# Batches 0 and 1 of an attention and channel-mixing kernel: q by runs of tokens, tokens rotated by one, v cast by its load, mixed weights in one step

## The chip, the cores and the metric

The kernel runs on one core of one Trainium2 chip. The metric is the device time of one execution in microseconds (us); where several runs are compared, the median counts.

## The reference

Linear attention, and then a channel-mixing layer that blends each token with the one before it. There are 8 batches of 576 tokens, 8 heads of 64 features, so 512 features a token, and 1024 hidden features.

```python
q_s = softmax(q, over the 64 features of a head)      # each token by itself
k_s = softmax(k, over the 576 tokens)                 # each feature by itself
kv  = einsum('bhsd,bhse->bhde', k_s, v)                # 64x64 a head
x   = q_s @ kv, heads side by side                    # (8, 576, 512)

x_prev = x moved by one token, zero first
xk = mu_k * x + (1 - mu_k) * x_prev
xr = mu_r * x + (1 - mu_r) * x_prev
k  = relu(xk @ w_k)
v  = (k * k) @ w_v
out = sigmoid(xr @ w_r) * v
```

Inputs and output are float32; the kernel multiplies in bfloat16 and adds up in float32.

## The kernel before

**Tiling.** A batch is worked on in two groups g (0 and 1). A group holds the heads 2g, 2g+1, 2g+4 and 2g+5: one pair of heads lies on the two halves of the 128 partitions (the code's r), the other pair is the second half of the free dimension (u). Each partition holds nine tokens in a row (j = 0 to 8), so token t is at partition t // 9, run j = t % 9, and after the transposes column 64 j + t // 9. A neighbour in time is thus 64 columns away, except for j = 0, whose predecessor is run 8, one partition up: a small copy, the edge, puts those 63 columns in front.

**Attention of batches 0 and 1 ("fused").** For batch b and group g the operations are, by the names that stand in the order list: `load` q, k and v (two halves n by u); `expq`, `rsum`, `rrec`, `scale` make softmaxed q (`qs`); `T` transposes it on PE into PSUM, and `qt` copies it to SBUF, one half by ACT and one by DVE; `edge` copies the last 63 columns to the front; `expk` makes exp of k; `KV` multiplies it with v on PE, and `Z` (a column of ones) gives the sums for k's softmax in batch 0, while in batch 1 a 65th column of v does that; `rz` is the reciprocal; `kvn` divides; `wp` multiplies kv by mu and by 1-mu, so that `X` on PE gives the mixed xk (m = 0) and xr (m = 1) straight away, in two parts t of 288 tokens; `x` copies them out to `xk` or `xr`. Batch 0's v is loaded with a cast to bfloat16 into a tile `vbs`, batch 1's v is loaded as float32 and cast on GpSimd (`cast`).

**Attention of batches 2 to 7** makes x plain and mixes it on DVE (`TKV`, `B`, `X` on PE, `diff`, `sc`, `mix` on DVE). It isn't touched but for its places in the order.

**Channel mixing.** Columns are taken in units (`UNITS`, two rings of 2304 tokens). For unit i and hidden tile fc, `k{i}_{fc}` multiplies xk with w_k, `relu` on ACT and `sq` on DVE square it. A unit of 256 columns takes two hidden tiles in one PSUM bank. In the early units each k is split in two: the first half needs group 0's xk and w_k tile `wk{h}0`, the second (".2") group 1's and `wk{h}1`. For each tile m of 128 tokens, `r{m}` multiplies xr with w_r, `th` is the tanh that gives the sigmoid, `v{m}_{part}` multiplies with w_v, `o` gates, `st` stores. PSUM has four banks `mm` for these and two pairs `att` for attention; a slot `any` is an `att` pair or two `mm` banks.

**The order.** Every engine works its instructions strictly in the order of one list written out by hand, `ORDER`. A token `name:2` puts the result in buffer 2, `name^other` makes it wait for another operation, `ACT!name` puts it on that engine. A buffer is given again only when its last user is done. `fill` is a matmul of zeros that nobody reads. Each engine's queue blocks at its first waiting instruction. Loads of batch 0 are on the DMA queues of SP and ACT, the weights and later batches on GpSimd's (POOL); stores are on SP.

Of the kernel before, what the change touches and what calls it, by code (L numbers as in the profile page):

```python
# [24 lines left out]
UNITS = (((0, 256), (256, 320), (576, 448), (1024, 512), (1536, 512), (2048, 256)),  # L25
# [4 lines left out]
         "kvn": 2, "wp": 2, "xb": 2, "xd": 2, "xm": 3, "rel": 3, "th": 10,  # L30
# [9 lines left out]
FUSED = (0, 1)  # L40
CROSS = (5, 6, 7)
EARLY_UNITS = 3
# [3 lines left out]
ident SP!load00q0:0 ACT!load00q1 zero ACT!load01q1:1 SP!load01q0 consts ACT!load00k1:2 SP!load00k0  # L46
late ACT!load01k1:3 SP!load01k0 warm fill:0 fill.2:1 fill.3:2 SP!rows expq000:0 expq001
load00v^expq000 rsum000:0 rsum001 load01v SP!muload expq010:1 rrec000 expq011 wk00 rrec001
scale000:0 fill.4^rrec001:3 fill.5^expq011:0 wk01 expk001:0 rsum010:1 fill.6^scale000:1 wk10
fill.7^scale000:2 expk000 scale001 load11q0:4 Z00:0 rrec010 rsum011 T00 expk010:1 load10q1:5 mu:0  # L50
wide:1 expk011 wk11 mucopy qt001:0 rrec011 qt000 scale011:1 load10q0 widecopy KV000 KV001 rest
Z01:1 rz00:0 fill.8^scale011:3 kvn00:0 fill.9^rz00:0 edge00 scale010 load11v0:6 KV010 KV011
wp001:0 T01 wp000 X0010:3 rz01:1 X0001:2 x0010 wr kvn01:1 X0000:0 wp010:1 qt010:1 wp011
fill.10^kvn01:3 x0000a qt011 load11k1:7 x0001a edge01 X0101:3 x0000b X0100:1 x0101a x0101b X0011:0
x0100a x0001b load11q1 k0_0:2 k0_2:3 x0100b k1_0:0 x0011 load11v1 expq110:2 k0_0.2 k1_3:1 k0_1
rsum110:2 wv0 expq101:0 k0_2.2 X0111:1 relu0_0:0 rsum101:3 k1_3.2 k1_0.2 relu1_3:1 k0_4:2
load10v1:8 x0111 k0_3 relu1_0:2 k0_4.2 k1_5:1 expq100 load11k0 sq1_3 k1_7:0 sq1_0 k0_5 rrec101
relu0_2:1 cast110:0 scale101:2 X0110:0 relu0_4:2 k1_4:3 sq0_0 k1_7.2 x0110 k1_5.2 sq0_2 k1_4.2
relu1_7:0 sq0_4 k1_1:2 relu1_5:1 k1_2:0 k1_1.2 k0_6:1 relu1_1:2 k1_2.2 k0_6.2 sq1_1 r1:2 rsum100
relu1_4:2 r0:3 sq1_4 th1:0 rrec100 rrec110 relu1_2:2 cast111 k0_7 th0:1 k1_6:2 sq1_2 load10k0:9  # L60
r2:0 scale100 expk111:2 wv1 scale110:0 k1_6.2 th2:2 r3:3 load10k1 expq111 load10v0 T10:1 th3:3
rsum111 wv2 v0_0:0 relu1_6:2 sq1_5 cast101:1 rrec111 sq1_7 v3_0:3 expk110 load20q0:10 scale111
expk100:0 load20v0:0 qt101:2 KV11:0 T11 sq1_6 relu0_6:1 load21q0:1 v1_0:2 rz11:2 qt110:0
load30q0:2 v0_1 qt100 kvn11:0 v3_1 expk101 edge10 sq0_6 v1_1 cast100 wp110:0 load20k0:3 qt111 KV10
edge11 X1101:0 rz10:0 load21k0:5 kvn10:1 v0_2 wp100:1 v3_2 wp111 o0 v1_2 o3 wp101 expq200:1
X1000:1 X1001:2 x1101 v2_0:3 load21v0:6 x1000 x1001 load30k0:4 cast200:2 X1111:0 o1 X1110:1
X1100:2 load30v0:7 rsum200:0 v2_1 x1100 load40k0:9 k2_7:2 expq210:0 v2_2 load31q0:8 k2_1:0 o2
k2_7.2 x1110 load51k0:10 k2_4:1 rsum210:1 expq300:2 k2_5:3 k2_1.2 k2_4.2 load31v0:0 rrec200
relu2_1:0 k2_5.2 x1111 relu2_7:2 X1010:1 sq2_1 expk200:1 X1011:0 k2_6:0 x1011 load40q0:1 k2_2:2
relu2_5:1 k2_6.2 scale200:1 k2_2.2 relu2_4:0 k2_0:3 load31k0:2 cast210:0 k2_3:1 sq2_7 k2_0.2 sq2_4  # L70
x1010 k2_3.2 sq2_5 rsum300:3 load41q0:3 TKV20:0 relu2_0:2 relu2_2:0 r5:3 relu2_3:1 rz20:1 sq2_0
load70q0:6 expk210:2 rrec300 r6:2 sq2_2 sq2_3 rrec210 r4:1 relu2_6:2 w20:0 scale210:2 load41v0:5
qt20:1 r7:0 th6:4 scale300:0 B21:1.0 expq310:1 v6_0:2 rz21:2 sq2_6 th7:5 load50k0:8 rsum310:2
xs20:0 r8:0 xb20 v6_1 rrec310 th4:6 w21:1 edge20 qt21:0 diff20:0 v4_0:1 o6 th5:7 X21:0.1 sc2001:0
v7_0:2 scale310:1 xs21:1 xb21 v5_0:3 cast300:1 sc2000 edge21 v4_1 diff21:1 v5_1 expk300:0
load60v0:7 sc2111:1 sc2101:2 v4_2 sc2100 th8:8 v7_1 load41k0:4 mix200 cast310:2 mix210 TKV30:1 o4
expq400:0 load51v0:0 k3_1:0 o5 k3_0:1 sc2010:0 load40v0:1 relu3_1:0 st5 rz30:0 sc2011 expq410:2
st6.2 rsum400:0 k3_3:3 st5.2 k3_2:0 relu3_0:1 load51q0:3 st4 sq3_1 relu3_3:2 w30:2 k3_7:1 rrec400
relu3_2:0 sc2110 sq3_0 expk310:1 k3_6:3 o7 sq3_2 st7.2 k3_5:0 qt30:2 sq3_3 load50v0:2 st3.2 mix211
k3_4:2 st6 relu3_7:1 rsum410:1 expk400:2 st0.2 B31:0.1 st3 sq3_7 relu3_4:0 mix201 st4.2 load50q0:9  # L80
v9_0:1 relu3_5:2 relu3_6:1 r9:2 sq3_5 scale400:2 xb30:1 v8_0:0 xs30 cast400:0 v10_0:3 sq3_6 sq3_4
edge30 rz31:1 v8_1 th9:9 w31:0 load71v0:1 diff30:0 qt31:1 r10:2 sc3001:2 sc3010:1 o8 B40:1.0
th10:7 sc3000 sc3011 r12:0 xb31:0 rz40:2 mix300 r11:2 rrec410 th12:4 mix301 xs31 v9_1 edge31
th11:3 diff31:1 expk410:0 v11_0:0 sc3101:0 sc3100 v10_1 expq510:1 o9 load60k0:4 mix310 v11_1
expq500:0 load70k0:3 rsum510:3 k4_7:2 load61k0:9 k4_4:1 o11 relu4_7:2 rrec510 expk500:1 scale410:0
k4_0:0 k4_3:2 relu4_4:1 load60q0:8 sq4_7 relu4_0:0 o10 k4_5:1 expq700:2 sc3111:2 st10 sq4_0 k4_1:0
sq4_4 st8.2 relu4_5:2 load70v0:6 sc3110 k5_0:3 st2 sq4_5 relu4_1:0 k4_6:1 rsum500:2 st7 cast500:1
st2.2 k4_2:0 relu4_3:1 w40:1 load71k0:2 k5_1 relu4_6:2 sq4_3 k5_6:2 sq4_1 relu5_0:1 k5_4:1 mix311
relu4_2:0 k5_7 expk510:2 r13:3 sq4_2 scale510:1 k5_5 relu5_6:0 load71q0:10 v12_0:0 th13:6 sq4_6
rrec500 cast410:2 v15_0:2 rsum700:0 v12_1 relu5_4:2 load61v0:5 sq5_6 expq600:1 k5_2:3 o12 r14:1  # L90
qt40:0 scale500:2 load61q0:8 st12 v14_0:0 cast510:0 rsum600:1 k5_3 tq50:2 v14_1 st0 th14:5 rrec600
# [93 lines left out]
def graph(kn):  # L185
# [40 lines left out]
    for g in range(2):  # L226
        vdone.append(add("POOL", lambda g=g: emit_v(g), name=f"load0{g}v"))
# [659 lines left out]
```

## Time and profile before

| | us |
|---|---|
| median of 3 runs | 199.8 (199.44 to 199.93) |
| the profiled execution | 199.27 |
| its span in the trace | 197.3 |
| PE busy | 184.6 |
| DVE busy | 152.3 |
| ACT busy | 134.6 |
| POOL busy | 44.9 |

The span is the time from the first to the last instruction of the trace; 1.97 us lie around it. The granted clock was 0.996 over the span. Of the columns of the profile's rows by time, the first is the start in us from the start of the span, the second the duration; PEld is the load of weights on TensorE, which goes on beside its matmuls; an arrow in brackets names what ended the idle time before the row. In the profile's names `eq` and `ek` are the exps of q and k, `qs` and `qt` q scaled and transposed, `raw` the loaded tiles, `xd` (shared with `vbs`) batch 0's v, `rel` relu's output, `k` the squares, `th` the tanhs and then the output.

### The profile page before, as it was taken

Reading aid. Unit: us, or ns where it says so; the run is one execution under the profiler, and the core shown is the slowest. Engines: PE = TensorE matmul, PEld = TensorE weight load, DVE = VectorE, ACT = ScalarE, POOL = GpSimd, SP = SyncE. Lnnn points to the kernel's source line nnn. Section 1 sums busy time; section 2 is a strip of 40 time slices with the busy share of each in tenths; the row PEclk is TensorE's granted clock in tenths of the full one; section 3 lists DMA queues with packets and bytes.
Section 4 is the critical chain, followed back from the end, with each engine's and each line's share of the span. In section 5 each row is a group of like instructions: output and inputs, shape, how many; then the busy total and the mean of one; then the engine's idle time right before and its main releaser. Section 6 shows DMA issues by size and latency. Waiting matters only on the chain.

```text
span 197.3 us, 4725 instructions
## 1 busy us (share of the span) xinstructions
PE 184.6 (94%) x1869; PEld 93.7 (47%) x1893; DVE 152.3 (77%) x347; ACT 134.6 (68%) x213; POOL 44.9 (23%) x72
## 2 busy tenths in 40 slices
PE   2599999899999999999999999999999999999991
PEld 0255665445444455446545664444444444444451
DVE  1877949799999999998989998999989245524421
ACT  3735778579999899889959999784187323742120
POOL 1855378695312421142400000000000000000000
PEclk9999999999999999999999999999999999999998
DMA  6999999999999999299998933496140041504735
GB/s 205 335 201 323 296 280 250 402 392 388 392 389 312 365 370 382 91 324 305 347 280 226 156 82 81 55 176 137 32 105 0 0 108 30 133 0 106 178 91 160
DMA packets 23598, 41.87 MB, mean 212 GB/s; under 512 B 9356, under 2 KB 12696, under 8 KB 23576
## 3 DMA queue, kind: packets, MB, share of 16 engines
q0 software_dynamic: 9376, 27.99, 44.5%
q1 hardware_dynamic: 13384, 12.14, 25.7%
q10 hardware_dynamic: 816, 1.44, 2.2%
q8 instruction: 15, 0.25, 0.5%
q14 instruction: 7, 0.06, 0.1%
HBM read 33.56 MB, written 9.44 MB: 218 GB/s over the span
## 4 chain that ended last, share of the span: by engine, by line
PE 84%; DVE 6%; ACT 3%; DMA 3%; issue 1%; ACTq 0%
PE mm_a L721 9%; PE mm_b L668 8%; PE mm_b L721 8%; PE mm_c L668 7%; PE mm_a L668 7%; PE mm_d L668 7%; PE mm_d L721 7%; PE mm_c L721 6%; PE mm_c L701 5%; PE mm_d L701 4%; PE mm_a L701 4%; DMA raw_c<-in_k_dram 3%; PE mm_b L701 2%; DVE k L657 1%; PE att_b L407 1%
## 5 line engine op out<-in xcount | busy, mean ns | idle before, releaser
L721 PEld LDWEIGHTS <-k 128*128 128x128 bf16 x296 | 27.9, 98 | 31.3 <-issue 0.9
L701 PEld LDWEIGHTS <-xr 128*128 128x128 bf16 x144 | 13.8, 98 | 15.0 <-issue 0.2
L657 DVE TENSOR_TENSOR k<-rel_c 128x512 bf16<-128x512 bf16 (+2 forms) x28 | 11.6, 415 | 9.3 <-ACT rel_c L647 9.2
L657 DVE TENSOR_TENSOR k<-rel_b 128x512 bf16<-128x512 bf16 (+2 forms) x23 | 9.6, 416 | 5.0 <-ACT rel_b L647 5.0
L647 ACT ACTIVATE rel_c<-mm_c 128x512 bf16<-128x512 f32 (+2 forms) x11 | 6.2, 563 | 9.0 <-PE mm_c L668 6.8
L701 PE MATMUL mm_c<-wr,xr 128*128 128x512 bf16 x47 | 12.3, 379 | 0.1
L668 PEld LDWEIGHTS <-wk_ba 128*128 128x128 bf16 x88 | 8.4, 98 | 7.9 <-issue 0.4
L668 PEld LDWEIGHTS <-wk_aa 128*128 128x128 bf16 x88 | 8.5, 98 | 7.8 <-issue 0.2
L668 PEld LDWEIGHTS <-wk_bb 128*128 128x128 bf16 x88 | 8.6, 98 | 7.2
L668 PEld LDWEIGHTS <-wk_ab 128*128 128x128 bf16 x88 | 8.5, 98 | 7.1 <-issue 0.2
L721 PE MATMUL mm_a<-wv_a,k 128*128 128x512 bf16 x44 | 11.3, 379 | 0.1
L657 DVE TENSOR_TENSOR k<-rel_a 128x512 bf16<-128x512 bf16 (+2 forms) x25 | 10.1, 405 | 1.3 <-ACT rel_a L647 1.3
L701 PE MATMUL mm_d<-wr,xr 128*128 128x512 bf16 x38 | 10.2, 379 | 0.1
L721 PE MATMUL mm_d<-wv_a,k 128*128 128x512 bf16 x36 | 9.2, 379 | 0.2 <-DVE th_d L727 0.2
L647 ACT ACTIVATE rel_b<-mm_b 128x512 bf16<-128x512 f32 (+2 forms) x11 | 6.3, 569 | 4.1 <-PE mm_b L668 4.1
L721 PE MATMUL mm_b<-wv_a,k 128*128 128x512 bf16 (+1 forms) x33 | 8.7, 367 | 0.2
L701 PE MATMUL mm_a<-wr,xr 128*128 128x512 bf16 x31 | 8.2, 380 | 0.1
L668 PE MATMUL mm_b<-xk,wk_bb 128*128 128x512 bf16 (+3 forms) x29 | 7.6, 342 | 0.1
L721 PE MATMUL mm_c<-wv_a,k 128*128 128x512 bf16 (+1 forms) x30 | 7.5, 366 | 0.2 <-issue 0.2
L668 PE MATMUL mm_b<-xk,wk_ba 128*128 128x512 bf16 (+3 forms) x29 | 7.6, 342 | 0.0
L647 ACT ACTIVATE rel_a<-mm_d 128x512 bf16<-128x512 f32 x5 | 3.0, 600 | 5.9 <-PE mm_d L668 5.9
L668 PE MATMUL mm_a<-xk,wk_ab 128*128 128x512 bf16 (+3 forms) x26 | 6.9, 348 | 0.1
(351 smaller groups left out, 499.8 us busy)
## 6 DMA issues: line engine op xcount, KB each, us to landing
raw_a<-in_v_dram POOLq DMA_DIRECT2D x3, 576.0 KB, 7.5
raw_e<-in_k_dram POOLq DMA_DIRECT2D x3, 576.0 KB, 4.7
raw_i<-in_q_dram POOLq DMA_DIRECT2D x3, 576.0 KB, 6.9
out_dram<-th_c SPq DMA_DIRECT2D x10, 128.0 KB, 2.5
raw_k<-in_q_dram POOLq DMA_DIRECT2D x2, 576.0 KB, 5.9
raw_b<-in_q_dram POOLq DMA_DIRECT2D x2, 576.0 KB, 10.3
raw_d<-in_k_dram POOLq DMA_DIRECT2D x2, 576.0 KB, 7.4
raw_g<-in_v_dram POOLq DMA_DIRECT2D x2, 576.0 KB, 7.1
```

Of the source, the lines that this page charges most:

```text
L407: kn.nc.tensor.matmul(kn.half(slot, r)[two[u], KVO:KVO + n], lhsT=kn.eks[ek.index][two[r], j, u, :], rhs=by, start=(j == 0), stop=(j == J ...
L647: kn.nc.scalar.activation(out=kn.rels[rel.index][:, 0:width], in_=kn.bank(kf)[:, 0:width], func=ACT.Relu, scale=HALF_ROOT)
L657: kn.nc.vector.tensor_tensor(out=to, in0=src, in1=src, op=ALU.mult)
L668: kn.nc.tensor.matmul(kn.bank(kf)[:, lo:lo + n], lhsT=kn.wk[fc // 4][ct % 2][:, ct // 2, (fc % 4) * 128: (fc % 4) * 128 + 128], rhs=kn.xs[ ...
L701: kn.nc.tensor.matmul(kn.bank(rps), lhsT=kn.xs[1][:, ct, c:c + 128], rhs=kn.wr[:, ct, :], start=(ct == 0), stop=(ct == CT - 1))
L721: kn.nc.tensor.matmul(kn.bank(vps)[:, 0:width], lhsT=kn.k2[:, ft, at:at + 128], rhs=wv_of(ft)[:, part], start=(ft == 0), stop=(ft == FT - 1))
```

## The change

- **q by runs.** In batches 0 and 1, q is loaded, exponentiated, summed, scaled, transposed and copied in two parts by runs of tokens, j = 0 to 4 and j = 5 to 8, for both u at once, in place of two parts by u.
- **Tokens rotated by one run.** X now takes the runs j = 1 to 4 first (256 columns, whose predecessors are j = 0 to 3), then j = 5 to 8 and j = 0 (320 columns, as 256 and 64). So its first part needs only q's first five runs and no edge; the edge copy now makes the predecessors of j = 0 at the end of the tile. The stores of batches 0 and 1 put the runs back in their places (`store`: j + 1 modulo 9).
- **Batch 1's v** is loaded with a cast into batch 0's v tile, and its `cast` on GpSimd goes; batch 1 has `Z` as batch 0, and its KV is split by u.
- **Mixed weights in one step.** `kvn` goes; `wp` takes kv from PSUM, the reciprocal as a scalar and mu in one instruction for each r.
- **Units.** The unit of 448 columns becomes 256 and 192, both with two hidden tiles a bank, and four units are early instead of three.
- **Orders.** The whole list is new. At its head: fifteen fills in a row; q's first runs of both groups and one k half on ACT's queue, the other k halves on SP's; the small mu rows on POOL's, ahead of v; q's remaining runs of batch 0 on POOL's, behind v and ahead of w_k. `qt` is DVE's unless the list says ACT (three of batch 1's), and several x copies are given to ACT.

```diff
-UNITS = (((0, 256), (256, 320), (576, 448), (1024, 512), (1536, 512), (2048, 256)),
+UNITS = (((0, 256), (256, 320), (576, 256), (832, 192), (1024, 512), (1536, 512), (2048, 256)),
+RUNS = (slice(0, 5), slice(5, J))
+PARTS = ((0, 256), (256, 320))
-EARLY_UNITS = 3
+EARLY_UNITS = 4
...
+ident ACT!load00q0:0 SP!load00k0:1 zero ACT!load01q0:2 SP!load00k1 fill:0 fill.2:1 fill.3:2
+fill.4:3 fill.5:0 fill.6:1 fill.7:2 fill.8:3 fill.9:0 fill.10:1 fill.11:2 fill.12:3 fill.13:0
+fill.14:1 POOL!rows consts ACT!load01k1:3 SP!load01k0 late warm POOL!muload expk000:0
+load00v^expk000 expq000:0 load01v expk001 rsum000:0 POOL!load01q1 expk010:1 rrec000 POOL!load00q1
+wide:0 scale000:0 expq010:1 wk00 expk011 rsum010:1 T000:0 wk01 widecopy Z00:1 Z01:3 rrec010
+qt000:0 load11q0:4 mu:1 fill.15^rrec010:0 scale010:1 fill.16^qt000:0 fill.17^qt000:0 load10q0:5
+rz00:0 rest T010:0 KV000 wk10 rz01:1 qt010:1 KV001 fill.18^rz01:0 wp000:0 fill.19^qt010:0
+fill.20^qt010:0 wp001 KV011 load11q1 KV010 X0000:0 wp010:1 expq011 load10k0:6 fill.21^qt010:0
+wp011 X0100:1 load10q1 expq001 rsum011 X0110:3 ACT!x0000b fill.22^expq011:0 rsum001
+fill.23^expq001:0 x0000a x0100a X0010:0 wk11 mucopy ACT!x0100b rrec011 rrec001 k0_0:0 scale011
+x0110 k0_2:1 x0010 scale001 T011:1 wr k0_2.2 qt011 T001:3 k0_0.2 edge01 load10k1 expq110:2 qt001
+X0111:0 X0101:1 edge00 X0001:3 load10v ACT!x0101b k0_1 x0001b x0001a k0_3 x0101a x0111 k1_1:2
...
+        if b in FUSED and i == 0:
+            us, runs = [slice(0, 2)] * 2, RUNS
...
+    def emit_v(b, g):
+        ap = bass.AP(tensor=kn.v.tensor, offset=kn.v.offset + (b * H + 2 * g) * S * D,
                      ap=[[J * D, 128], [4 * S * D, 2], [1, J * D]])
         return kn.nc.gpsimd.dma_start(out=kn.vbs[g][:], in_=ap)
...
+            to = kn.qts[qt.index]
+            copy = kn.nc.vector.tensor_copy if op and op[0].engine == "DVE" else kn.nc.scalar.copy
+            cols = slice(64 * js.start, 64 * js.stop) if js else slice(0, S)
+            place = cols if js else slice(64, 64 + S)
...
             if b == 0:
+                vdone[1, g].deps += kvm
...
-                return kn.nc.vector.tensor_copy(out=t[:, :, 1:64], in_=t[:, :, 576:639])
+                return kn.nc.vector.tensor_copy(out=t[:, :, S + 1:S + 64],
+                                                in_=t[:, :, S - 64:S - 1])
...
+            def mixed_weights(m):
+                for r in range(2):
+                    c = 256 * m + 128 * g + 64 * r
+                    made = kn.nc.vector.scalar_tensor_tensor(
+                        out=kn.wps[wp.index][:, m, :, two[r]],
+                        in0=kn.half(kvp, r)[:, None, KVO:KVO + 64].to_broadcast((128, 2, 64)),
+                        scalar=kn.rzs[rz.index][:, r:r + 1], in1=kn.mu_wide[:, :, c:c + 64],
+                        op0=ALU.mult, op1=ALU.mult)
...
+                pieces = (((64, 0, 0, 256),) if t == 0 else
+                          ((320, 256, 0, 256), (0, S, 256, 64)))
+                for now, before, to, n in pieces:
+                    for i, at in enumerate((now, before)):
...
-        pair = n == 256
+        pair = n <= 256
...
+                if bb in FUSED:
+                    j = (j + 1) % J
```

More of the change, by code (lines that the diff above doesn't have):

```diff
@@ L40 @@
 FUSED = (0, 1)
+RUNS = (slice(0, 5), slice(5, J))
+PARTS = ((0, 256), (256, 320))
 CROSS = (5, 6, 7)
-EARLY_UNITS = 3
+EARLY_UNITS = 4
 ALONE = ((2, 1), (B - 1, 1))
 ORDER = """
[L46 to L67, printed above, removed]
@@ new lines @@
+relu0_2:0 k1_3:3 load11k1:7 k1_1.2 rsum110:2 relu0_0:1 k1_2:1 wv0 k1_3.2 relu1_1:2 sq0_2 k1_0:0
+k1_2.2 rrec110 load11k0 relu1_3:0 sq0_0 k0_4:2 k1_0.2 expq111 sq1_1 scale110:2 load11v X0011:1
+relu1_2:1 k1_4:3 relu1_0:2 k1_6:1 x0011 expq100:1 k1_5:0 k1_6.2 load20q0:8 sq1_3 expq101 k0_4.2
+sq1_2 T110:0 rsum111 relu1_6:0 k1_4.2 k0_5 rsum100:3 relu1_4:1 k0_6:1 k1_5.2 k0_6.2 sq1_0 k1_7:3
+sq1_4 k0_7 relu1_5:2 rrec111 k1_7.2 wv1 sq1_6 relu0_4:1 r2:0 scale111 relu1_7:0 wv2 rsum101 T111:1
+th2:0 r1:2 rrec100 rrec101 scale100:1 ACT!qt110:2 r3:3 load30q0:9 expk101:2 scale101 ACT!qt111
@@ new lines @@
+load21q0:10 sq0_4 T101:0 r0:0 relu0_6:1 expk100 sq0_6 KV101:1 qt101:1 th0:1 Z10 edge11 sq1_7 KV100
+th3:2 T100:0 rz10:2 edge10 v3_0:1 load21k0:1 expk111:0 sq1_5 wp101:1 ACT!qt100 load20v0:3 wp100
+v1_0:0 expk110 X1000:1 Z11:0 x1000 load20k0:2 KV110 KV111 th1:3 v2_0:3 rz11:0 wp110:0 wp111
+load21v0:0 expq200:0 X1100:1 k2_2:2 DVE!x1100 X1011:0 X1001:1 x1011 load31q0:4 k2_2.2 ACT!x1001
+v3_1 rsum200:1 k2_3 load51q0:5 X1101:0 relu2_2:1 X1111:1 ACT!x1101 rrec200 k2_0:2 x1111 v3_2
+k2_0.2 expq300:2 load40k0:6 v2_1 o3 k2_1 scale200:0 v1_1 relu2_0:0 k3_0:1 v2_2 load31k0:7
@@ L315, in graph @@
         for g in range(2):
-            for n in range(3):
+            for n in range(2 if b in FUSED else 3):
                 load(b, g, n)
@@ L489, in qedge @@
             def qedge():
                 t = kn.qts[qt.index]
-                return kn.nc.vector.tensor_copy(out=t[:, :, 1:64], in_=t[:, :, 576:639])
-            qdone = add("DVE", qedge, qcopy + [consts], name=f"edge{tag}")
-            def mixed_weights(op, m):
-                for i in range(2):
-                    (kn.nc.gpsimd if op[0].engine == "POOL" else kn.nc.vector).tensor_tensor(
-                        out=kn.wps[wp.index][:, m, i, :],
-                        in0=kn.kvns[kvn.index][:].rearrange("p a e -> p (a e)"),
-                        in1=kn.mu_wide[:, i, 256 * m + 128 * g:256 * m + 128 * g + 128],
-                        op=ALU.mult)
@@ new lines, in attention @@
+            qdone = add("DVE", qedge, [qcopy[1], consts], name=f"edge{tag}")
+            def mixed_weights(m):
+                for r in range(2):
+                    c = 256 * m + 128 * g + 64 * r
[4 more added lines that the diff above has]
+                        op0=ALU.mult, op1=ALU.mult)
+                return made
@@ new lines, in mixed_x @@
+            def mixed_x(m, t, slot):
+                pieces = (((64, 0, 0, 256),) if t == 0 else
+                          ((320, 256, 0, 256), (0, S, 256, 64)))
+                for now, before, to, n in pieces:
+                    for i, at in enumerate((now, before)):
+                        for r in range(2):
+                            for u in range(2):
+                                kn.nc.tensor.matmul(
+                                    kn.half(slot, u)[two[r], to:to + n],
+                                    lhsT=kn.wps[wp.index][two[u], m, i, two[r]],
+                                    rhs=kn.qts[qt.index][two[u], r, at:at + n],
+                                    start=(i == 0), stop=(i == 1))
@@ L521, in out_x @@
                 else:
                     for u in range(2):
[L523 to L524 removed]
+                        copy(out=kn.xs[m][:, g + 2 * u, c:c + n],
+                             in_=kn.half(slot, u)[:, 0:n])
             for m in range(2):
[L527 to L528 removed]
+                made = add("DVE", lambda m=m: mixed_weights(m), [zdone, wide_done] + kvm, [wp],
+                           [kvp, rz], name=f"wp{tag}{m}")
```

292 lines of the change are left out of this document (147 added, 145 removed).

## The prediction

> **What bounds the kernel now.** I read the page's busy shares and slices first, then busy time by stretch, then the timeline of the first 43 us, since the edits lie there.
>
> ```profile
> PE 184.6 (94%) x1869; PEld 93.7 (47%) x1893; DVE 152.3 (77%) x347; ACT 134.6 (68%) x213; POOL 44.9 (23%) x72
> PE   2599999899999999999999999999999999999991
> ...
> 19.17:42.84 23.67, 22.47 (x282) 13.18 (x283) 19.91 (x48) 17.12 (x33) 16.41 (x27) 1.00 1.08 318
> 50.00:190.00 140.00, 138.47 (x1317) 68.44 (x1335) 111.56 (x243) 99.62 (x152) 14.45 (x20) 1.00 0.63 183
> ```
>
> A row by stretch gives its length, then busy us of PE, PEld, DVE, ACT and POOL, the granted clock, the share of the DMA engines and GB/s. PE is the bound: from 50 to 190 us it is idle for 1.5 us of 140, from 19.17 to 42.84 for 1.2 us. So the time is: when the channel-mixing matmuls start, plus PE's work, plus its few waits. Only three things can move it: the start, added PE work, new waits. The DMA engines are full up to 43 us (1.08), so the loads' order is a limit as well.
>
> ```profile
> 19.17 0.39 PE L668 MATMUL mm_c<-xk,wk_aa 128*128 128x256 bf16 x2
> 42.84 0.54 PE L668 MATMUL mm_c<-xk,wk_ba 128*128 128x448 bf16 x2
> 18.19 0.20 DVE L491 COPY qt_b<-qt_b 128x126 bf16<-128x126 bf16 x1
> 18.30 0.45 DVE L518 CAST xk<-att_a 128x288 bf16<-128x288 f32 x1
> ```
>
> The first k matmul is at 19.17, the first of unit 2 (batch 1) at 42.84. The DVE's last edge copy, which the old order needs before that first k, ends at 18.39.
>
> **Start of the new order, walked by hand.** Loads first.
>
> ```profile
> 4.54 1.25 ACT L333 ACTIVATE eq_a<-raw_a 128x576 bf16<-128x576 f32 x2 [0.25 <-DMA raw_a<-in_q_dram]
> 5.96 1.25 ACT L333 ACTIVATE eq_b<-raw_b 128x576 bf16<-128x576 f32 x2 [0.16 <-DMA raw_b<-in_q_dram]
> 7.70 1.26 ACT L333 ACTIVATE ek_a<-raw_c 128x576 bf16<-128x576 f32 x2 [0.49 <-DMA raw_c<-in_k_dram]
> 9.34 1.26 ACT L333 ACTIVATE ek_b<-raw_d 128x576 bf16<-128x576 f32 x2 [0.38 <-DMA raw_d<-in_k_dram]
> 11.62 0.56 POOL L209 DMA_DIRECT2D raw_f<-in_q_dram  x1 [0.52 <-DMA xd_a<-in_v_dram]
> 12.99 0.54 POOL L209 DMA_DIRECT2D raw_g<-in_v_dram  x1 [0.82 <-DMA xd_b<-in_v_dram]
> 14.27 0.75 POOL L307 DMA_DIRECT2D wr<-in_moe_w_r_dram  x1 [0.74 <-DMA wk_aa<-in_moe_w_k_dram]
> 15.61 0.54 POOL L209 DMA_DIRECT2D raw_h<-in_k_dram  x1 [0.59 <-DMA wk_ab<-in_moe_w_k_dram]
> ```
>
> Each row starts when the load behind the arrow has landed. SP's and ACT's queues deliver two 288 KB halves per 1.6 us; POOL's queue delivers 576 KB of f32 v in 1.37 us, 512 KB of f32 w_k in 1.3. The change puts q's first five runs (320 KB) and k on the quick queues: q0 and k0 at 4.6, k's second half 6.0, group 1's k 7.7. The four-run remainders of q go on POOL behind both v loads. Summed at those rates POOL's queue lands: v0 11.3, v1 12.7, remainders 13.4 and 14.0, wk00 15.3, wk01 16.6, wk10 19.6, wk11 22.9, wr 25.5, batch 1's v 27.7 and 33.2, wv0 31.0, wv1 36.0, wv2 37.3. The mu rows are now POOL's, ahead of v; v stays held by the first exp (k's now), about where it was. A v load of batch 1 reads the same f32 bytes, so its cast by the load saves no DMA time; it takes four casts off POOL, whose queue then no longer stops for their data. It adds a wait: the tile is batch 0's v tile, so POOL's queue waits there for KV000 and KV001 (12.3), but that load stands 14 loads behind, at about 20, and nothing behind it is held. Now the durations.
>
> ```profile
> 22.63 0.69 ACT L333 ACTIVATE eq_a<-raw_f 128x576 bf16<-128x576 f32 x1
> 23.21 0.60 ACT L647 ACTIVATE rel_b<-mm_d 128x512 bf16<-128x512 f32 x1
> 25.13 0.45 ACT L647 ACTIVATE rel_a<-mm_a 128x320 bf16<-128x320 f32 x1
> 25.46 0.45 ACT L647 ACTIVATE rel_b<-mm_b 128x320 bf16<-128x320 f32 x1
> ...
> 8.96 0.70 DVE L348 TENSOR_REDUCE rsum_b<-eq_b 128x9 f32<-128x576 bf16 x1
> 10.24 0.45 DVE L383 COPY qt_a<-att_a 128x576 bf16<-128x576 bf16 x1
> 10.60 0.20 DVE L352 RECIPROCAL rrec_b<-rsum_b 128x9 f32<-128x9 f32 x1
> 10.84 0.76 DVE L357 TENSOR_TENSOR qs_b<-eq_b,rrec_b 128x576 bf16<-128x576 bf16 x1
> 12.68 0.43 DVE L283 TENSOR_SCALAR mu_wide<-mu_wide 128x512 f32<-128x512 f32 x1 [1.08 <-ACT mu_wide L287]
> 13.02 0.16 DVE L414 RECIPROCAL rz_a<-att_a 128x2 f32<-128x2 f32 x1
> 13.22 0.29 DVE L424 TENSOR_TENSOR kvn_a<-att_a,rz_a 128x128 f32<-128x128 f32 x1
> 14.19 0.89 DVE L497 TENSOR_TENSOR wp_a<-kvn_a,mu_wide 128x128 bf16<-128x128 f32 x4
> 39.26 0.68 DVE L727 SCALAR_TENSOR_TENSOR th_b<-th_b,mm_a 128x512 f32<-128x512 f32 x1
> ```
>
> ACT's next instruction starts before the last one's end: 0.58 after a 0.69 exp, 0.33 after a 0.45 relu. I walk queues by such steps (about 0.1 less than the duration) and dependences by durations, scaled by elements: 640 columns of the five runs 1.1 times 576, 512 of the four runs 0.9 times.
>
> ACT: expk000 4.6, expq000 5.2, expk001 6.0, expk010 7.7, expq010 8.3, ready 9.05. DVE from 9.1: rsum010 0.82, rrec010 0.2, qt000 0.5, scale010 0.8, rz00, rest, rz01 0.75 in all, qt010 0.5: to 12.35. The new mixed weights, two instructions from PSUM each, are not in the trace: the old wp took 0.22 an instruction from SBUF, the only such form, th_b's, 0.68 for four times the columns. I take 0.24 (nearest in columns; at 0.35 all eight cost 0.9 more; less than 0.22 is excluded by as many columns). That replaces kvn and wp, 0.29+0.45 a group, by 0.96: dearer for DVE, one step shorter in dependence (batch 1's second weights, so far POOL's, come to DVE too: 0.45 a group, where it has slack at 30 us). wp000 and wp001 end at 13.3. wp010 waits for KV010, for which PE has T010, KV000, KV001, three fills (18 to 20), KV011 and KV010 in its queue: 13.4 at full clock. wp010 and wp011 end at 14.4. Behind them, rsum011, rsum001, two reciprocals, two scales, two qt copies, two edges: 18.4. So DVE's last edge comes no earlier than today.
>
> What is gained is that k no longer waits for it. X0000 runs at 13.4, X0100 14.05, X0110, X0010 to 15.45; x0000b and x0000a stand on ACT behind expq011 and expq001, which wait for the remainders (14.0), and end at 15.45. **First k at 15.5, not 19.17.** Then PE waits for scale011 (1.0 us idle before T011), T001 and the edges; by 20.35 it has done k0_0 to k0_3, k1_1, k1_3 and half of the next, 1.4 us more matmul than before at that time, and X0110 and X0111 too: 1.9 us ahead.
>
> **To unit 2.** The next bound is ACT, which feeds PE's four banks: from 19.9 to 33.7 it has eight 320-column relus, four double ones, tanhs, batch 1's exps and three qt copies (those on ACT by the new order), without a gap. Walked so, r2 ends at 27.4, r0 30.3, v3_0 starts at 31.6 (wv0 31.0), KV110 33.9 (its v 33.2), and k2_2 at 35.45. No load is late, the smallest margin 0.6.
>
> ```profile
> 53.68 0.86 PE mm_a L701 x4
> 18.39 0.53 PE L508 MATMUL att_b<-qt_b,wp_b 64*64 64x288 bf16 x8
> 33.72 0.48 PE L407 MATMUL att_a<-vv_a,ek_c 64*64 64x65 bf16 x36
> 17.81 0.45 PE L508 MATMUL mm_c<-qt_b,wp_b 64*64 64x288 bf16 x1
> 18.36 0.28 PE L508 MATMUL mm_c<-qt_b,wp_b 64*64 64x288 bf16 x1
> 7.38 0.63 PE L299 MATMUL mm_a<-rel_c 128*128 128x512 bf16 x1
> 7.81 0.63 PE L299 MATMUL mm_b<-rel_c 128*128 128x512 bf16 x1
> ```
>
> But the states differ: the new order still owes nine v parts of batch 0 (4.3 us at 0.43 per two 512-column pairs of weights, 0.86 per four) where the old owed one (0.43), and six X (two of 256 columns, 0.24; four of 256+64, 0.36: 1.9) where the old owed two (0.5): 5.3 us. The old kernel's equal point is 42.84-5.3=37.55, so the lead is **2.1 us**. It holds the added work already: Z for batch 1, 2 x 0.3 us, and the 64-column pieces, eight matmuls at 13 ns (the KV row: 36 in 0.48), 0.1 each. By the Trainium skill (TensorE: Matmul & The Clock Gate, "Wait — 56ns, not 53.3ns?") start to start never falls below some 25 ns, which would make each 0.2 and the sum 0.4 later; here the KV row speaks against it, as its matmuls take quarters of the array. Splitting unit 2 into 256 and 192 adds no columns: nothing, as 128x256 streams at the rate of 512 (0.22 to 0.11); if weight loads showed, 32 more at up to 0.1 would be 3 us, but today's loads lie beside the matmuls (PEld 47% busy).
>
> Behind unit 2 PE's work is the old one in a new order. Its waits from 50 to 190 are 1.5 us today; I allow half as much again, +0.7 (from -0.7 to +1.5).
>
> **Sum.** The profiled execution took 199.27 (span 197.3, 1.97 around it); the median of the three runs is 0.53 above. 199.27-2.1+0.7=197.9; as a median **198.4 us**. About 0.3% (0.6 us) is what a measurement of this kernel can tell from no change: faster is below 199.2, slower above 200.4.
>
> **Rivals.** *The slow clock (slower).* The fills start 0.43 us apart, and an X matmul's duration falls from 0.45 to 0.28 only at 18.3: PE ran at half speed until then though never idle for a us from 7 on. The fifteen fills at the start, at 0.43 some 6 us in one piece, are more unbroken work of the whole array than the old order has anywhere ahead of 18.3, so I take full speed from there; but from 8 to 11.4 the walk has PE busy for only half the time. If it falls back, fills 18 to 20 and four KV halves cost twice, wp011 ends at 16.0, the whole DVE queue 1.6 later, and the first k matmuls lose 0.9: 198.4+2.5=200.9. It decides at KV010: after 14.5 the gain is gone. By the Trainium skill (same page, "What's actually happening") a busy window of about 3.4 us lifts the gate and an idle one lowers it; read literally PE never idles so long, and the forecast stands. The trace shows that patchy work didn't lift it, so patchy work may not hold it either. Chance 0.2.
>
> *ACT as the bound (no change).* If ACT's 32 instructions from 19.9 to k2_2 take durations instead of steps (0.05 more each, as many wait for PE), 1.6 go: 200.0. For it: eight copies moved to ACT. Against: the steps are measured. Chance 0.2, spread around no change.
>
> *The loads (slower).* q now comes in pieces of 1280 and 1024 bytes a row, not 2304, and four weights land within 1.3 us of their use. If POOL's queue is 7% slower, wv0 and batch 1's v are 2 us late and all but 0.6 of it shows, and TKV20, walked at 46.9 with its k at 44.8, is late too: some 2.3 us: 200.7. The rows bound each piece's cost only from one side. Chance 0.15.
>
> **How the numbers follow.** Forecast 0.45. Faster 0.45; same 0.18 (the ACT case, less a little); slower 0.37 (clock, loads, and that little). Range: down to 197.0 (order waits fewer by 0.7, so 198.4-1.4), up to 201.2 (the clock case with some worse waits). The forecast's own range is 197.0 to 199.2.
>
> **What would show it.** First k at 15 to 16; fills 18 to 20 0.22 apart; the last edge near 18.4; k2_2 near 35.5; PE idle between first k and k2_2 of about 1.4 us; from 50 to 190 about 2.2. Wrong if the X matmuls at 13 to 15 us last 0.45, or if the first k comes after 17.5, or if PE waits for wv or for batch 1's and 2's loads.

## The result, and the profile after

The changed kernel took **201.41 us** (median of 13 runs, 200.31 to 203.29) where the kernel before took 199.80 in the same series (13 runs, 199.33 to 200.74). The ratio is 1.0080, with an interval from 1.0057 to 1.0103: slower by 0.8%. The forecast was 198.4 us, faster than before, with a range of 197.0 to 201.2.

The profiled execution took 200.31 (span 198.5), which is the shortest of the thirteen. The page, in the lines that the prediction showed of before:

```profile
PE 191.8 (97%) x2038; PEld 98.9 (50%) x2038; DVE 151.6 (76%) x347; ACT 135.0 (68%) x213; POOL 44.1 (22%) x68
...
PE   7799999999999999999999999999999999999992
...
PEclk9969999999999999999999999999999999999999
```

PE is busier by 7.2 us than in the trace of before, 3.7 of them in the first 16 us and 1.4 from 50 to 190, where the trace of before lacks records of matmuls (more on that below). The third slice of the granted clock reads 6. The rows by stretch (length, then busy us of PE, PEld, DVE, ACT and POOL, the granted clock, DMA share, GB/s) give its place:

```profile
10.00:12.00 2.00, 2.00 (x20) 0.79 (x18) 1.75 (x7) 0.07 (x1) 1.59 (x3) 0.50 1.08 319
12.00:14.00 2.00, 2.00 (x49) 1.23 (x49) 1.50 (x5) 1.26 (x2) 1.67 (x3) 0.65 1.24 212
...
20.00:50.00 30.00, 29.81 (x412) 18.85 (x408) 25.28 (x57) 24.95 (x44) 14.79 (x21) 1.00 1.11 327
50.00:190.00 140.00, 139.91 (x1345) 69.19 (x1345) 112.08 (x242) 98.42 (x150) 14.45 (x20) 1.00 0.62 178
```

By the trace's clock records TensorE got full speed at 6.57, lost it at 9.98 for 3.41 us, and had it again from 13.40. The timeline shows what ran there (start, duration, engine, line, operation):

```profile
10.19 1.46 PE L310 MATMUL mm_a<-rel_c 128*128 128x512 bf16 x3
...
11.96 0.99 PE L419 MATMUL att_b<-xd_a,ek_a 64*64 64x64 bf16 x36
...
12.99 1.13 DVE L524 SCALAR_TENSOR_TENSOR wp_a<-att_b,rz_a,mu_wide 128x128 bf16<-128x128 f32 x4 [0.43 <-PE att_b L419]
...
14.56 0.35 DVE L524 SCALAR_TENSOR_TENSOR wp_b<-mm_c,rz_b,mu_wide 128x128 bf16<-128x128 f32 x1 [0.44 <-PE mm_d L419]
...
16.96 0.39 PE L702 MATMUL mm_a<-xk,wk_aa 128*128 128x256 bf16 x2
...
19.38 0.29 DVE L516 COPY qt_a<-qt_a 128x126 bf16<-128x126 bf16 x1
...
37.86 0.39 PE L702 MATMUL mm_c<-xk,wk_aa 128*128 128x256 bf16 x2
```

DVE waits twice for PE, 0.43 and 0.44 us, ahead of the mixed weights. The first k is at 16.96 (15.5 forecast), the last edge ends at 19.67 (18.4), unit 2 starts at 37.86 (35.45). The equal point of the old kernel was put at 37.55, so the lead of 2.1 us is not there. PE itself hardly waits after that: it is idle for 0.2 us between 20 and 50 and for 0.09 from 50 to 190. Its longest waits are all in the head (line, for whom, us in total, times, longest):

```profile
PE mm_a L310 <- DVE qt_c L257: 1.2, 1, 1.2
PE mm_a L280 <- DMA mu_rows<-in_moe_mu_r_dram: 0.6, 1, 0.6
PE mm_c L406 <- ACT ek_b L344: 0.5, 1, 0.5
PE att_b L387 <- DVE qs_b L369: 0.3, 1, 0.3
```

The first is ahead of all fills, the second at 7.04, the third at 9.20, the last at 17.57.

In other runs the half speed lasted longer. Runs with a mean clock of 0.989 to 0.991 had spans of 198.5 to 199.2, those with 0.982 or 0.983 had 199.3 to 200.6, one with 0.980 had 201.5. Half of 3.41 us in 198.5 is 0.009 and twice that 0.017, so most runs spent about 6.8 us at half speed, twice as long as the profiled one. That is why the median lies 1.1 us above the profiled time.

### The profile page after: what moved, and what is told of

The parts are those of the page before. It is cut to its first block, busy times and chain, and to the rows that moved or that the text cites. A ratio compares the mean times of both kernels' runs of the same rounds, so it can differ in the third digit from the quotient of the medians.

```text
span 198.5 us, 5051 instructions
## 1 busy us (share of the span) xinstructions
PE 191.8 (97%) x2038; PEld 98.9 (50%) x2038; DVE 151.6 (76%) x347; ACT 135.0 (68%) x213; POOL 44.1 (22%) x68
## 4 chain that ended last, share of the span: by engine, by line
PE 90%; DMA 3%; DVE 3%; ACT 1%; SPq 0%; issue 0%; DVEq 0%; ACTq 0%
PE mm_b L755 10%; PE mm_a L702 9%; PE mm_c L702 9%; PE mm_c L755 8%; PE mm_b L702 8%; PE mm_d L755 7%; PE mm_d L702 7%; PE mm_a L755 6%; PE mm_a L735 5%; PE mm_d L735 5%; PE mm_c L735 3%; DMA raw_d<-in_k_dram 3%; PE mm_b L735 3%; PE att_b L419 2%; PE att_a L419 2%; PE att_a L387 1%
## 5 line engine op out<-in xcount | busy, mean ns | idle before, releaser
L735 PEld LDWEIGHTS <-xr 128*128 128x128 bf16 x144 | 13.6, 98 | 15.7 <-issue 0.2
L735 PE MATMUL mm_a<-wr,xr 128*128 128x512 bf16 x48 | 12.3, 379 | 0.0
L755 PE MATMUL mm_c<-wv_a,k 128*128 128x512 bf16 x36 | 9.2, 379 | 0.0
L755 PE MATMUL mm_d<-wv_a,k 128*128 128x512 bf16 (+1 forms) x36 | 8.8, 368 | 0.0
L702 PE MATMUL mm_a<-xk,wk_ba 128*128 128x512 bf16 (+3 forms) x30 | 7.4, 328 | 0.0
L702 PE MATMUL mm_b<-xk,wk_ab 128*128 128x512 bf16 (+3 forms) x30 | 7.4, 328 | 0.0
L702 PE MATMUL mm_a<-xk,wk_bb 128*128 128x512 bf16 (+3 forms) x30 | 7.4, 328 | 0.0
L702 PE MATMUL mm_b<-xk,wk_aa 128*128 128x512 bf16 (+3 forms) x30 | 7.4, 327 | 0.0
L683 ACT ACTIVATE rel_b<-mm_d 128x512 bf16<-128x512 f32 (+2 forms) x6 | 3.3, 558 | 5.8 <-PE mm_d L702 5.8
L735 PE MATMUL mm_c<-wr,xr 128*128 128x512 bf16 x28 | 7.2, 380 | 0.0
L755 PE MATMUL mm_a<-wv_a,k 128*128 128x512 bf16 x28 | 7.2, 379 | 0.0
```

Source lines behind the costliest of these rows:

```text
L683: kn.nc.scalar.activation(out=to, in_=src, func=ACT.Relu, scale=HALF_ROOT)
L702: kn.nc.tensor.matmul(kn.bank(kf)[:, lo:lo + n], lhsT=kn.wk[fc // 4][ct % 2][:, ct // 2, (fc % 4) * 128: (fc % 4) * 128 + 128], rhs=kn.xs[ ...
L735: kn.nc.tensor.matmul(kn.bank(rps), lhsT=kn.xs[1][:, ct, c:c + 128], rhs=kn.wr[:, ct, :], start=(ct == 0), stop=(ct == CT - 1))
L755: kn.nc.tensor.matmul(kn.bank(vps)[:, 0:width], lhsT=kn.k2[:, ft, at:at + 128], rhs=wv_of(ft)[:, part], start=(ft == 0), stop=(ft == FT - 1))
```

## The experiments

The experiments ran in three series, and the kernel before ran in each. Its medians were 199.66, 199.51 and 199.98, so kernels of different series are compared by their ratios to it.

**A warm clock** (e1_warm: eight more matmuls of zeros, nothing else).

```diff
- ... fill.14:1 POOL!rows consts ...
+ ... fill.14:1 fill.24:2 fill.25:3 fill.26:2 POOL!rows consts ...
- wide:0 scale000:0 ...     fill.15^rrec010:0 scale010:1
+ wide:0 fill.27:1 fill.28:1 fill.29:1 scale000:0 ...     fill.15^rrec010:0 fill.30:0 fill.31:0 scale010:1
```

> The changed kernel with eight more fills at the head (three before wide, three behind it, two behind fill.15), so that PE has no stretch with little in it from 6.9 to 11.3 us. Theory C (the clock that falls back from 10 to 13.4 us costs the gain): the granted clock stays at 1.0 to the end, T010 to KV010 take half as long, wp011 ends near 14.5 instead of 15.6, first k near 15.7, and the time falls by 1.0 to 1.8 us, to 199.6-200.4. Theory W (the gain is eaten by more PE work from 20 to 50 us, the clock only shifts idle time at the start): first k comes earlier, but PE waits for the loads and ACT then, and the time stays within 0.4 us of 201.4.

It took 199.82 us; the ratio to before is 1.0006 (0.9983 to 1.0029), against 1.0080. In the profile the clock rose at 5.9 and stayed, by the rows by stretch and the timeline:

```profile
10.00:12.00 2.00, 2.00 (x36) 1.07 (x38) 1.97 (x8) 0.40 (x1) 1.34 (x2) 1.00 1.11 314
12.00:14.00 2.00, 2.00 (x85) 1.37 (x83) 1.69 (x8) 1.14 (x2) 1.51 (x3) 1.00 1.22 215
```

```profile
11.95 0.66 PE L419 MATMUL att_b<-xd_a,ek_a 64*64 64x64 bf16 x36
...
13.99 0.35 DVE L524 SCALAR_TENSOR_TENSOR wp_b<-mm_c,rz_b,mu_wide 128x128 bf16<-128x128 f32 x1 [0.21 <-PE mm_d L419]
14.25 0.34 DVE L524 SCALAR_TENSOR_TENSOR wp_b<-mm_d,rz_b,mu_wide 128x128 bf16<-128x128 f32 x1
...
16.39 0.39 PE L702 MATMUL mm_a<-xk,wk_aa 128*128 128x256 bf16 x2
```

So the fall of the clock costs 1.5 us of the median (0.74% of 199.8), and 0.5 in the two profiled executions (200.31 and 199.78), since the fall was short in that one. The eight fills don't always hold it: in nine of the twelve runs the mean clock was 0.996 or more and the median 199.64 us, in three it was 0.989 or 0.990, and they took 200.87 to 201.18. And the first k came to 16.39 only (15.7 expected), and unit 2 to 37.29 (its row stands further down): with a full clock the forecast lead still isn't there.

**Three fills in place of fifteen** (e2_fewfills).

```diff
- fill:0 fill.2:1 fill.3:2
- fill.4:3 fill.5:0 ... fill.13:0 fill.14:1
+ fill:0 fill.2:1 fill.3:2
```

> The changed kernel with three fills at the head instead of fifteen. Theory C: PE is at half speed from the start to about 17 us instead of for 3.4 us of it, first k 0.5 to 1 us later than 16.96, the time 0.3 to 1.0 us longer, 201.7-202.4. Theory W: no change beyond 0.4 us, since the DVE's queue, not PE, sets the first 20 us.

201.23 us, 1.0061 (1.0040 to 1.0083): not told from the changed kernel. The clock rose at 14.0, the first k came at 17.46. The twelve fills buy an early rise that is lost again before it is of use; the expected loss did not come.

**Less small work**, one edit each: batch 1's Z as two matmuls of the eighteen (e3_z_short, which leaves most of the sum over tokens out), and X's second part as one piece of 320 columns (e4_x_whole, which takes columns a run off).

```diff
-             for j in range(J):
+             js = 1 if b else J
+             for j in range(js):
```

```diff
-                           ((320, 256, 0, 256), (0, S, 256, 64)))
+                           ((256, 192, 0, 320),))
```

> The changed kernel with batch 1's Z cut from 18 matmuls a group to 2 (the sums for k's softmax are then those of one run of tokens). Theory W: PE is full from 20 to 50 us, so 32 matmuls fewer, 0.5 us by the trace, come off the time: 200.8-201.0. Theory C: no change beyond 0.3 us, as Z lies where PE has slack.

> The changed kernel with X's second part as one piece of 320 columns (eight matmuls) instead of 256 and 64 (sixteen); it takes columns that are a run off, so the mix is of other tokens. Theory W: eight parts of that kind shorter by 0.1 us each, four of them ahead of 20 us: the time falls by 0.3 to 0.6, to 200.8-201.1. Theory C: within 0.3 us of 201.4.

200.66 us, 1.0028 (1.0006 to 1.0051), and 200.88, 1.0049 (1.0027 to 1.0071). Each looked like 0.5 us or more of added work. But half speed lasted 6.83 us in e3's profile and 3.41 in e4's, so the clock blurs both. Among runs of a mean clock of 0.978 to 0.983 the medians are 201.54 (changed kernel), 200.70 (e3) and 201.06 (e4), among those near 0.99 they are 200.74, 200.07 and 200.05, and the kernel before was 0.14 lower in this series than beside the changed kernel. So at the same clock some 0.5 to 0.7 us are left for e3 and 0.3 to 0.6 for e4. The kernels that follow correct this reading too, as a cut also moves where instructions are fetched.

**Both, with the warm clock** (e7_warm_less: the edits of e1, e3 and e4 together).

> The kernel with the eight more fills (first experiment), and both cuts on it: batch 1's Z with 2 of 18 matmuls a group, X's second part in one piece of 320 columns (columns a run off). Theory W, that clock and added PE work are separate prices that add up: 199.8 less 0.6 less 0.4, 198.6-199.1, which is below the kernel before. If instead the clock was all and the cuts only filled its gaps, the cuts bring nothing here: 199.6-199.9.

This missed: 200.86 us, 1.0070 (1.0043 to 1.0097), slower than the warm kernel with all its work. The chain of waits from 50 us on (start, length, what) shows a hole that no profile so far had at that place:

```profile
52.96 0.31 PE att_a L387 x36
53.27 0.28 PE att_a L420 x33
53.55 1.40 issue
54.95 0.22 PE att_a L420 x3
```

PE stands for 1.40 us after 33 of the 36 small matmuls of a K and v product, at an instruction that waits for no semaphore. A 16 KB transfer of instructions landed 0.11 us into that time. I counted TensorE's instructions in all the traces (weight loads, matmuls and the four to six drains and semaphore waits among them) against these transfers. As far as the traces' records are whole, they run in blocks of 256: number 449 + 256 j is the last of a block. Never did the next one start sooner than 1.28 us after its transfer had landed, and in three rows of this table PE stood still until then:

| kernel | j | transfer | first of the block at | after landing | PE stood |
|---|---|---|---|---|---|
| warm, less work (e7) | 4 | 52.53 to 53.66 | 54.95 | 1.29 | 1.40 |
| before, warm (e5) | 0 | 16.01 to 16.94 | 18.46 | 1.52 | 0.55 |
| warm (e1) | 7 | 74.41 to 75.35 | 76.64 | 1.28 | 0.2 |
| after | 5 | 54.34 to 55.39 | 61.44 | 6.05 | none |

Taking work out had moved the end of a block into the run of small matmuls. By the Trainium skill (Runtime: NRT & Kernel Launch, "Instruction fetch mechanics") instructions come in blocks of 16 KiB, 256 of them, and the fetch is mostly hidden, as dispatch is slower than the fill. The size agrees with the count here; that it is hidden doesn't hold where some 36 pairs of instructions go by in 0.6 us.

**Blocks shifted** (e9_less_shifted is e7, e11_warm_shifted is e1; only the head differs, with 22 pairs in e9, as shown, and 33 in e11, and both leave out fill.5).

```diff
-         def fill(slot=slot):
+         def fill(slot=slot, i=i):
+             if i == 0:
+                 for _ in range(22):
+                     kn.nc.tensor.matmul(kn.bank(slot)[:, 0:8], lhsT=kn.still[:, 0:128],
+                                         rhs=kn.still[:, 0:8], start=True, stop=True)
```

> The kernel with the warm clock, batch 1's Z of two matmuls and X's second part in one piece, with 22 pairs of weight load and 8-column matmul put into the first fill and one other fill left out: the same work behind the head, but each block of TensorE's instructions ends 42 instructions earlier in the program. In the profiles so far the weight loads and matmuls stand in blocks of 256, one ends at number 449 + 256 j, and the first of the next block never starts sooner than 1.28 us after its block's transfer (about 1 us, 16 KB) has landed; where that was short TensorE stood still. Theory F (fetch): the 1.40 us stand at 53.55 us was that. Moved by 42, number 1473 falls where the transfer is asked for among 512-column matmuls, so the stand goes, no other takes its place, and the prices of clock (1.6 us) and of small work (about 1.1) add up to 198.6 to 199.4. Rival N: the stand is due to something at that place (the K and v product waits for a port or for v), and stays: 200.5 to 201.0. Rival O: cutting Z and X under a warm clock moves a wait elsewhere: the stand goes, but the time stays above 199.8.

> The kernel with the warm clock alone (199.82 us), with 33 such pairs in the first fill and one other fill left out: each block ends 64 instructions earlier, nothing behind the head is changed. Theory F: now a block's end falls among the 36 pairs of the K and v product at 54 us, as it did in the kernel that missed, and TensorE stands 1.0 to 1.6 us there: 200.8 to 201.4. Rival N: pairs in the head are free, so nothing changes: 199.6 to 200.1, and no stand at 54 us.

e9 took 199.11 us, 0.9968 (0.9954 to 0.9982); e11 took 201.79, 1.0101 (1.0072 to 1.0130). In e9 42 instructions more cost nothing in the head (first k at 16.39, as in e1) and took 1.0% off; in e11 64 more put 1.0% on. In e9's chain the stretch runs through:

```profile
53.15 0.31 PE att_a L391 x36
53.46 0.30 PE att_a L424 x36
53.76 0.32 PE mm_d L740
```

and in e11's chain the hole stands where e7 had it, after 33 of 36, and another in the head:

```profile
16.86 0.73 issue
...
54.94 0.28 PE att_a L423 x33
55.22 1.79 issue
57.01 0.22 PE att_a L423 x3
```

So it is the fetch, and not the place in the program. By ratios e9 won 2.0 us on e7, more than the hole of 1.40, and the rest is open. e11 lost 1.9 to e1, more than expected, since only the hole of 1.79 was counted: in its profile (202.50 us, above its median) the added pairs also delay the fills, so that the X ahead of the first k starts at 16.56 and not 16.04, and the hole in the head adds 0.73. With the holes gone, e9 against e1 is the price of the work left out: 0.4% or 0.76 us by ratio, 0.63 by the last matmul of the two profiles (193.21 and 193.84). In these two profiles Z carries it, and X's split doesn't. A Z of eighteen takes 0.31 in e1 (31.86 to 32.17)

```profile
31.46 0.47 PE L419 MATMUL att_b<-xd_a,ek_c 64*64 64x64 bf16 x18
31.86 0.38 PE L406 MATMUL att_b<-one,ek_c 64*128 64x1 bf16 x18
32.17 0.47 PE L419 MATMUL att_b<-xd_a,ek_c 64*64 64x64 bf16 x18
```

and a Z of two 0.10 in e9, so two groups save 0.42. Two X parts in 256 and 64 columns take 1.00 and 0.82 us in e1 (from 37.62 and from 39.81 to the next k), and in 320 columns the same in e9. The other 0.2 of the 0.63 is what e1 loses at a block's end at 76.6. What e4 gained at the same clock isn't explained by this.

**Parts of the change on the kernel before.** Its clock rose at 18.33. e5_before_warm adds 23 fills; e8_before_cast casts batch 1's v by its load (with Z for batch 1, and no cast on GpSimd); e10_before_cast_warm does both.

```diff
- late ... warm fill:0 fill.2:1 fill.3:2 SP!rows
+ late ... warm fill:0 fill.2:1 fill.3:2 fill.11:1 ... fill.30:0 SP!rows
- wide:1 expk011 wk11 mucopy
+ wide:1 expk011 wk11 fill.31:2 fill.32:2 fill.33:2 mucopy
```

```diff
-     for g in range(2):
-         vdone.append(add("POOL", lambda g=g: emit_v(g), name=f"load0{g}v"))
+     for b in FUSED:
+         for g in range(2):
+             vdone[b, g] = add("POOL", lambda b=b, g=g: emit_v(b, g), name=f"load{b}{g}v")
...
+                 zm = add("PE", lambda: zs(kvp), expk + [consts], [kvp], [], name=f"Z{tag}")
```

> The kernel before with 23 more fills at its head (20 in one piece before the first exp is ready, 3 behind wide). Theory C (the clock of the first 18 us is worth more than a us, whatever the order): full speed from about 6 us, the second group's KV and T in half the time, the last edge copy 0.7 to 1.0 us earlier, first k near 18.2, time 198.6-199.1. The rival: DVE's queue sets the start in the old order, so first k stays at 19.0 or later and the time within 0.3 us of 199.7.

> The kernel before with one part of the change alone: batch 1's v is cast by its load into batch 0's v tile, GpSimd's four casts go, and batch 1 gets its Z matmuls. Theory W: Z adds 0.6 us of PE work, of which some is given back where GpSimd's casts and DVE met: 199.9-200.4. The rival (GpSimd's casts hold the load queue and PE waits for it at 30 to 40 us): 0.5 us faster, 199.0-199.4.

> The kernel before with two parts together that each alone did little: batch 1's v cast by its load (199.45 alone) and 23 more fills ahead (199.21 alone). If the parts add: 199.1 to 199.3. If the two free each other (less for GpSimd to do, an earlier start): 198.4 to 199.0, and that would beat both kernels. If a block of instructions ends in the head where TensorE is now early (number 449 cannot start before about 18.3 us with a transfer asked for at 16.0): 199.2 to 199.6 with a stand of 0.5 us at 17 to 18 us.

e5: 199.21 us, 0.9979 (0.9960 to 0.9998), between its two expectations. e8: 199.45, 0.9997 (0.9985 to 1.0009), no change, and so neither of its two. e10: **198.84, 0.9952 (0.9934 to 0.9969)**, which beats both kernels. In the old order the early clock is worth less: e5's first k moved from 19.17 to 18.82 only. The chain ahead of it goes through the copies of q on ACT and DVE until 16.96, and at 17.91 PE meets a block's end:

```profile
PE att_a L508 <- DVE qt_a L383: 1.2, 1, 1.2
PE att_a L508 <- issue: 0.6, 1, 0.6
```

(waits of PE: line, for whom, us in total, times, longest). e10 stands 0.41 us at that place. The first row is another wait, for batch 1's q at 37 us, and there e5 gives back part of what it won: 1.18 us, where before waits 0.73, and e8 and e10, with a Z of 0.3 us ahead of it, 0.36 and 0.31. The first three rows are of e5, the others of e10:

```profile
36.58 1.19 POOL L497 TENSOR_TENSOR wp_a<-kvn_a,mu_wide 128x128 bf16<-128x128 f32 x2
36.92 1.00 DVE L497 TENSOR_TENSOR wp_a<-kvn_a,mu_wide 128x128 bf16<-128x128 f32 x2
38.34 0.44 PE L508 MATMUL att_a<-qt_a,wp_a 64*64 64x288 bf16 x8 [1.18 <-DVE qt_a L383]
...
36.97 0.48 DVE L501 TENSOR_TENSOR wp_a<-kvn_a,mu_wide 128x128 bf16<-128x128 f32 x2
37.87 0.44 PE L512 MATMUL att_a<-qt_a,wp_a 64*64 64x288 bf16 x8 [0.31 <-DVE qt_a L384]
```

The DVE's two weights took 1.00 us in e5 while GpSimd, behind its cast, worked on its own two, and 0.48 in e10, where GpSimd had no cast and was done with its two by 36.77. That fits the two parts giving more together (0.48%) than one by one (0.24%), a difference that still lies within their intervals. e10 has neither q by runs, nor rotated tokens, nor the mixed weights in one step.

## Why the prediction was wrong, step by step

What failed is the lead of 2.1 us at unit 2. With the clock held (e1) it was 0.26 us, 37.29 against 37.55: the first k came 0.9 late, and another 0.95 were lost between it and unit 2, where the walk had too little work for PE. The clock, which the forecast took as held, cost 1.5 more in the median.

**The clock: the rival, by its own mechanism.** It was given 0.2. Patchy work did let the clock fall, at 9.98, and in the profile half of what was named came: the fills took 0.43 each (10.19, 1.46 for three), group 0's K and v product 0.99 instead of 0.66, but group 1's, at 13.87, ran at full clock again. The weights ended at 15.7 (16.0 in the rival, 14.4 in the forecast). The rival's price of 2.5 us was too high, and its 200.9 came near by luck: the clock costs 1.5, and the rest of the miss is other. The forecast leaned on the unbroken fifteen fills; e2 shows that twelve of them gain nothing. By the Trainium skill (TensorE: Matmul & The Clock Gate, "What's actually happening") an idle window of some 3.4 us throttles. Here the clock's records also come 3.41 us apart (6.57, 9.98, 13.40), but from 6.57 to 9.98 PE was idle for 1.07 us only, in pauses of 0.61 (at 7.04) and 0.46: much smaller pauses were enough.

**The start at full clock: 0.9 us too early.** With the clock held (e1) the first k is at 16.39, not 15.5. The q sum of group 1 starts 0.3 late (9.39 against 9.1), the mixed weights of group 1 end at 15.1 and not 14.4. The instruction's price isn't the cause: 0.26 from start to start (13.99 to 14.25) where 0.24 was taken. What came late was group 1's K and v product: the weights that wait for it start at 13.99, where 13.4 was walked. From there on to the first k it was not taken apart.

**X's price: a mis-sized term.** The prediction took 0.24 us for an X part of 256 columns and 0.36 for 256 and 64. In e1's rows

```profile
34.66 0.41 PE L538 MATMUL att_b<-qt_b,wp_b 64*64 64x256 bf16 x8
35.00 0.38 PE L406 MATMUL att_a<-one,ek_a 64*128 64x1 bf16 x18
...
36.87 0.49 PE L538 MATMUL att_b<-qt_c,wp_a 64*64 64x256 bf16 x8
37.29 0.39 PE L702 MATMUL mm_c<-xk,wk_aa 128*128 128x256 bf16 x2
37.62 0.47 PE L538 MATMUL att_a<-qt_b,wp_b 64*64 64x256 bf16 x16
38.22 0.47 PE L538 MATMUL att_b<-qt_b,wp_b 64*64 64x256 bf16 x16
38.62 0.39 PE L702 MATMUL mm_c<-xk,wk_ab 128*128 128x256 bf16 x2
...
46.37 0.41 PE L538 MATMUL att_a<-qt_b,wp_b 64*64 64x256 bf16 x8
46.61 0.39 PE L538 MATMUL att_b<-qt_c,wp_a 64*64 64x256 bf16 x8
46.93 0.34 PE L702 MATMUL mm_c<-xk,wk_aa 128*128 128x192 bf16 x2
```

one part of 256 takes 0.34 or 0.42 from its start to the next group, two 0.56, and two of the second form 1.00 (0.82 at 39.81). The trace of before would have told it:

```profile
21.13 0.44 PE L508 MATMUL att_b<-qt_b,wp_b 64*64 64x288 bf16 x8
21.50 0.45 PE L668 MATMUL mm_b<-xk,wk_ab 128*128 128x320 bf16 x2
```

0.37 us for 288 columns, start to start, where 0.25 was taken, besides 0.1 lost behind the 128-row matmul ahead of it. The six X still owed at unit 2 took 2.4 us in e1 (1.00, 0.82 and 0.56), not 1.9, and the old kernel's two 0.62, not 0.5. That makes the equal point some 0.35 earlier, or 0.55 with the tenth ahead of each group (three groups against one). The six X between the first k and unit 2 took 2.14 (0.97, 0.41, 0.34 and 0.42), 0.2 more than the same prices give. So X's price explains little of what was lost there.

**Added PE work: right.** Z at 0.3 each measured 0.31 and came out of the time again in e9. The 64-column pieces at 0.1 each cost at most that: in e9 their removal shortened nothing. Units of 256 and 192 columns cost next to nothing: in e1 their matmuls start 0.109 and 0.082 us apart, 0.191 together, where one of 448 columns takes 0.19 in before.

**ACT and the loads: not the bound, and PE's work too small.** PE was idle for 0.27 us between the first k and unit 2 where 1.4 was forecast; it waited neither for ACT, nor for w_k, w_v or batch 1's v. The v loads landed no later than walked. So the 19.95 us walked there (15.5 to 35.45) held 18.55 of work for PE, and the 20.90 in e1 held 20.63: the walk had 2.1 us too little work. X's price is 0.2 of that. In e1 PE also changes ten times there from a 128-row matmul to a group of small ones, and each time the group starts about 0.1 later than the next 128-row matmul would have, 1.1 in all; whether the walk had these isn't known, and the rest is open.

**Waits behind 50 us: a number without a base.** The +0.7 was half of "1.5 us of waits" in before. That trace holds 1869 matmuls beside 1893 weight loads, so 24 records are missing. From 50 to 190 us its idle time is 19 gaps, fourteen of 53 ns and five of 159, which make the whole 1.5. e5 has the same program behind its head, and its trace has all records:

```profile
50.00:190.00 140.00, 140.00 (x1336) 68.35 (x1334) 111.87 (x243) 99.98 (x153) 14.79 (x21) 1.00 0.62 182
```

So PE has no waits there in before. What the new order loses behind unit 2 (0.26 ahead there in e1, 0.79 behind at the start of the last matmul, 1.05 in all) is 0.35 to 0.55 of X's price by the count above and 0.2 at the block's end at 76.6; the rest is open. That the forecast's +0.7 is near is luck.

**The sum.** Against the profiled forecast of 197.9, the profile of e1 with 199.78 is 1.9 late: 0.9 at the first k, 0.95 to unit 2, 0.35 more than allowed behind it, less 0.3 because the last matmul's start lay nearer to the end of the run (5.94 us, 6.22 in before). The clock adds 0.5 in the profile of after, and in the median 1.5. The 0.95 is taken apart only as far as told above, and neither the rotation nor the mixed weights were tried alone.

## What to carry to other kernels

Price a group of small matmuls from the start of the group to the start of the next large one, not by the duration of one, and add what is lost ahead of the group. A lead in the head is only worth what the clock lets it be: ask for every stretch of 3.4 us ahead of the main work whether TensorE is busy without pauses, and fill those pauses, not the start. When a cut makes a kernel slower, look for a hole marked "issue" at a matmul that waits for nothing, and move the program by some dozens of instructions before believing that the cut was bad.

## What the runs showed of the hardware

- **Instruction blocks.** TensorE's instructions are fetched in blocks of 256 (16 KB in some 1 us), and in all the traces here the first of a block started 1.28 us or more after it landed. When the end of a block falls in a run of small matmuls (36 in 0.6 us), PE stands for 1.40 (e7) or 1.79 us (e11). 64 instructions added in the head made the one kernel 1.9 us longer (0.5 us of its profile is that the fills start later), 42 the other 2.0 shorter.
- **The clock falls without a long pause.** It fell for 3.41 us after 3.41 us in which PE was idle for 1.07, in pauses of 0.61 and 0.46 us amid matmuls of two rows, of one column or of 64, and in most runs it fell for about twice that. Eight 512-column matmuls of zeros in those places held it in nine runs of twelve.
- **Matmuls on a quarter of the array start closer than 25 ns apart.** The 36 of a K and v product ran in 0.59 us from its first to the next 128-row matmul (35.31 to 35.90 in e1), 16 ns each. The Trainium skill (TensorE: Matmul & The Clock Gate, "Wait — 56ns, not 53.3ns?") has some 25 ns as the least; these rows disagree.
